# Fourier kernel on one core: first DFT of the last two x tiles by column block, first chunk read in parts, each chunk read in one transfer

## The chip, the cores and the metric

The kernel runs on one NeuronCore of a Trainium2 chip. The core has TensorE (PE, matrix products into PSUM), VectorE (DVE), ScalarE (ACT), GpSimd (POOL) and SyncE (SP, here only an issuer of DMA transfers). ACT and POOL can issue transfers too. The metric is the device time of one execution in microseconds. All data is float32; much of the matrix work is done in pairs of a rounded "high" part and a "low" rest, in the type fp32r.

## What is computed

One block of a network with two halves, on x of shape [1, 1, 4096, 640]:

```python
mod = (silu(c) @ w_mod)                 # six rows of 640: sa, ca, ga, sb, cb, gb
h = layernorm(x) * (1 + ca) + sa
x = x + ga * A(h)                       # A: spectral mixing, below
h = layernorm(x) * (1 + cb) + sb
x = x + gb * ((silu(h @ w_gate) * (h @ w_up)) @ w_down)

def A(h):
    z = rfft2(h, axes=(1, 2))           # real DFT over the 4096 positions and the height of 1
    z = z.reshape(..., 4, 160)          # four blocks of 160 columns
    hr, hi = relu(complex product of z with w1[block] + b1)
    o = complex product of (hr, hi) with w2[block] + b2
    o = sign(o) * max(abs(o) - 0.01, 0) # on the real and the imaginary part
    return irfft2(o)
```

The feed-forward half has 1728 hidden columns.

## The kernel before

The DFT over 4096 positions is split as 128 by 32. Position n is n1*32 + n2, with n1 on the 128 partitions. x is loaded as eight tiles `xas[t]`, each with four values of n2 (called rows here) of 640 columns. For each tile the kernel takes the layernorm statistics (`ln_stats`, DVE and POOL), applies them in place (`ln_apply`, shared between ACT and DVE), and multiplies with the constant matrix `fa`, the DFT over n1 (`dft_a`). That is five products for each tile, of 512 columns each. Products 0 to 3 take one row each, the first 128 columns of all four blocks; product 4 takes the last 32 columns of each block ("remainder") of all four rows. The results are copied from PSUM back over the tile (`evac_a`): row i's columns 0 to 511, and 512 to 639 for the remainders.

After that the 128 partitions hold frequencies, interleaved so that f = 0, 1, 2 picks every fourth, every fourth, and every second partition. `write_s1(t, f)` writes tile t's part f to the DRAM buffer `s1[f]`, for later reading with n2 on the partitions. f = 0 serves the frequency chunks 0 and 1, f = 1 chunks 2 and 3, f = 2 chunks 4 to 7. f = 0 and 1 are 320 KB each for a tile, f = 2 is 640 KB.

`load_g(ch, lo, hi)` reads chunk ch's rows n2 from lo to hi back, into a tile `gs[ch]` of 128 partitions (4*n2 + q) by 4 by 640; two such tiles exist. It issues one transfer for each q, so four for a chunk. Chunk 0 is read in two steps: rows 0 to 27 by POOL's queue once tile 6 is written, rows 28 to 31 by SP's queue once tile 7 is.

Each of the eight chunks then goes through these stages:

- `stage_b(ch, t)`, written b(ch,t) below: the DFT over n2 for the column block t (t = 4 is the remainders), with the table `tb`, into a bank of PSUM. `evac_b` scales the result with `ca1` and splits it into a high part (ACT) and a low part (DVE), called z. For the remainders, chunk 0 has them copied into the tile `rz` by `evac_r` block by block (ACT, DVE); other chunks write them to DRAM (`rem_high`, `rem_low`, `rem_move`) and read them back (`rem_read`).
- `stage_l1(ch, b)`, written l1(ch,b): the product with w1 for block b, bias and relu, and `tail_l1` for its remainder columns.
- `stage_l2(ch, b)`, l2(ch,b): the product with w2. DVE adds the bias and writes the tile `tt`.
- `move_x`, shrinking, and `stage_i`, the inverse DFT over n2, written to the DRAM buffer `s2` by POOL.

The loop over p = 4*ch + b sets the order: in each turn l1 of this block, b of a block of the next chunk, l2 of the block before, and the inverse of a block further back. Every engine runs its instructions in the order in which the code issues them. What sits ahead in an engine's program waits ahead, and a transfer on a queue comes behind those issued on it before.

w1 and w2 are each split into tiles a, b, c with high and low columns. `prep_weights` lists the jobs, `weights_high` does a high part (ACT for w1, POOL for w2), `weights_low` the low part (DVE). w1 has twelve jobs, done after the first DFT; w2 has six, three of whose low parts come ahead of the loop and three at the end of turn p = 0.

The tiles `w2a`, `w2b`, `w2c` lie where tiles 1, 2 and 3 of x lay, and `tt` where tiles 4 and 5 lay, so they wait for all writes of those x tiles. SP's order behind the first DFT is chunk 1's read, a table, b2, the f = 1 writes of tiles 0, 4, 5, 6, 7, chunk 2's read, a table, and the f = 2 writes of the same tiles.

`first_scale`, `remainders` and `columns` compute `ca1` (1 + ca): five DVE operations, a copy, and ten small products. `idle(n)` issues n products whose result nobody reads, to keep TensorE's clock up. There are 54 of them behind `columns` and 8 ahead of block 2 of chunk 0.

The feed-forward half follows the loop, in an order that a planner writes out when the kernel is built; the change does not touch it.

## Time and profile before

| | us |
|---|---|
| time, median of 3 runs | 1463.02 (1460.88 to 1465.1) |
| the profiled execution's own time | 1461.29 |
| its span | 1459.5 |
| PE busy | 1416.4 (97%) |
| DVE busy | 1083.6 (74%) |
| ACT busy | 785.5 (54%) |
| POOL busy | 551.7 (38%) |
| PE starts its first product | 7.94 |
| last product of the first DFT ends | 48.98 |
| first product of chunk 0 | 63.61 |

In a profile line of the timeline, the first two numbers are the start and the length in us, then come the engine (PEld is TensorE's weight load, SPq the issue of a transfer by SP), the source line, the operation, what it writes and reads, the shapes and the count; behind it, in brackets, how long the engine had been idle and what released it. Consecutive instructions of one kind are merged in a line. Matmul counts are twice the products written in the code. In the view of busy time by stretch, a DMA share of 1 means that all 16 DMA engines were busy, and the clock is the granted share of TensorE's full clock.

### The profile page before, as it was taken

How to read it: one execution, taken by the hardware profiler on the slowest of the kernel's cores; microseconds unless marked ns; L12 is line 12 of the kernel's file. 1: busy time of each engine (PE TensorE's matmuls, PEld its weight loads, DVE VectorE, ACT ScalarE, POOL GpSimd, SP SyncE). 2: the span in 40 equal slices, each digit the busy share in tenths (PEclk: the TensorE clock that was granted, in tenths of full speed). 3: DMA queues.
4: the chain of work that ended last, by engine and by line, in shares of the span. 5: the costliest groups of instructions: out<-in, count | busy, mean ns of one | idle time of the engine just before them, and what ended most of it. 6: DMA issues, size and time to landing. Idle time of an engine off the chain costs nothing.

```text
span 1459.5 us, 24171 instructions
## 1 busy us (share of the span) xinstructions
PE 1416.4 (97%) x8628; PEld 1341.4 (92%) x8628; DVE 1083.6 (74%) x1963; ACT 785.5 (54%) x1554; POOL 551.7 (38%) x646
## 2 busy tenths in 40 slices
PE   6999999998999999999999999999999999999998
PEld 2799999966888888899999999999999999999998
DVE  8568877878797788757887768888747767567775
ACT  7658888744545555544565446555434444244432
POOL 5400100044655444322544424444324545046532
PEclk9999999999999999999999999999999999999999
DMA  9967767648677988798987997877696666966652
GB/s 379 338 215 228 232 199 219 220 145 275 235 276 267 337 293 279 274 364 291 314 271 248 342 367 254 310 246 249 237 345 219 222 215 238 352 212 232 205 188 83
DMA packets 184712, 380.07 MB, mean 260 GB/s; under 512 B 22480, under 2 KB 103056, under 8 KB 182544
## 3 DMA queue, kind: packets, MB, share of 16 engines
q1 hardware_dynamic: 176080, 360.99, 71.8%
q0 software_dynamic: 6928, 14.91, 3.3%
q10 hardware_dynamic: 1584, 2.62, 0.5%
q8 instruction: 68, 1.11, 0.3%
q14 instruction: 52, 0.43, 0.1%
HBM read 263.91 MB, written 105.39 MB: 253 GB/s over the span
## 4 chain that ended last, share of the span: by engine, by line
PE 61%; DVE 8%; DMA 4%; issue 2%; ACT 2%; POOL 1%; SPq 0%; POOLq 0%; DVEq 0%; ACTq 0%
PE pd L2269 12%; PE pw L1950 8%; PE pw L1948 8%; PE pw L1949 8%; PE pd_X L2129 4%; PE pg L1813 2%; PE pg L1812 2%; PE pg L1814 2%; PE pd_Y L2129 2%; PE pw L1959 2%; PE pw L1960 2%; PE pw L1961 2%; DMA cr<-s 2%; DVE wb L1266 2%; PE pd_Z L2129 1%
## 5 line engine op out<-in xcount | busy, mean ns | idle before, releaser
L2269 PE MATMUL pd<-wdh,a 128*128 128x320 f32 x1040 | 238.9, 310 | 1.5 <-DVE a L1849 1.3
L2269 PEld LDWEIGHTS pd<-wdh,a 128*128 128x128 f32 x1040 | 176.2, 188 | 2.5 <-DVE a L1849 1.6
L1266 DVE TENSOR_TENSOR wb<-r,wb 128x512 fp32r<-128x512 f32 (+3 forms) x156 | 159.8, 1032 | 16.3 <-ACT wb L1263 14.0
L2269 PE MATMUL pd<-wdl,a 128*128 128x320 f32 x540 | 166.3, 309 | 0.0
L1948 PE MATMUL pw<-h,wt 128*128 128x384 f32 x416 | 140.8, 339 | 3.1 <-ACT s_x L1967 2.1
L1950 PE MATMUL pw<-h,wt 128*128 128x384 f32 x416 | 140.4, 338 | 0.0
L1949 PE MATMUL pw<-h,wt 128*128 128x384 f32 x416 | 139.9, 336 | 0.0
L1263 ACT ACTIVATE wb<-r 128x512 fp32r<-128x512 f32 (+3 forms) x172 | 117.9, 703 | 32.8 <-PE pw L1961 24.8
L2241 DVE TENSOR_TENSOR x<-x,pd 128x320 f32<-128x320 f32 x240 | 108.9, 477 | 35.7 <-PE pd L2269 32.1
L1950 PE MATMUL pw<-h,wb 128*128 128x384 f32 x312 | 105.1, 337 | 2.3 <-DVE wb L1266 2.3
L1948 PE MATMUL pw<-h,wb 128*128 128x384 f32 x312 | 105.5, 338 | 0.0
L1949 PE MATMUL pw<-h,wb 128*128 128x384 f32 x312 | 105.0, 337 | 0.0
L1812 PE MATMUL pg<-ht,wb 128*128 128x512 f32 x260 | 102.8, 396 | 1.3 <-ACT wb L1263 1.3
L1814 PE MATMUL pg<-ht,wb 128*128 128x512 f32 x260 | 101.7, 391 | 2.2 <-DVE wb L1266 2.2
L2269 PEld LDWEIGHTS pd<-wdl,a 128*128 128x128 f32 x540 | 101.4, 188 | 0.5
L1813 PE MATMUL pg<-ht,wb 128*128 128x512 f32 x260 | 101.5, 390 | 0.0
L742 POOL DMA_DIRECT2D s<-co x28 | 15.5, 555 | 190.8 <-ACT co L741 183.0
L1967 ACT ACTIVATE s_x<-pw 128x384 f32<-128x384 f32 x52 | 25.4, 489 | 113.6 <-PE pw L1950 112.9
L1525 POOL TENSOR_TENSOR cr<-cr,gab 128x640 f32<-128x640 f32 x28 | 47.5, 1696 | 100.5 <-DMA cr<-s 89.6
L1948 PEld LDWEIGHTS pw<-h,wt 128*128 128x128 f32 x416 | 78.3, 188 | 4.7 <-ACT s_x L1967 3.1
L1949 PEld LDWEIGHTS pw<-h,wt 128*128 128x128 f32 x416 | 78.3, 188 | 0.0
L1950 PEld LDWEIGHTS pw<-h,wt 128*128 128x128 f32 x416 | 78.3, 188 | 0.0
(335 smaller groups left out, 4079.0 us busy)
## 6 DMA issues: line engine op xcount, KB each, us to landing
wt<-td SPq DMA_DIRECT2D x104, 512.0 KB, 5.3
hs<-ho SPq DMA_DIRECT2D x52, 512.0 KB, 5.5
h<-hs SPq DMA_DIRECT2D x32, 768.0 KB, 7.9
r<-in_B_w_gate_dram SPq DMA_DIRECT2D x36, 640.0 KB, 4.8
r<-in_B_w_up_dram SPq DMA_DIRECT2D x36, 640.0 KB, 5.0
wdr<-wdd SPq DMA_DIRECT2D x21, 640.0 KB, 5.2
td<-wt SPq DMA_DIRECT2D x25, 512.0 KB, 6.0
g<-s SPq DMA_DIRECT2D x28, 320.0 KB, 5.9
```

What stands on the lines that cost most here:

```text
L1263: act.activation(wbs[t, n][:, 0, ks, e], raw[t, n][:, ks, e], AF.Copy)
L1266: (pool if onp else dve).tensor_tensor(wbs[t, n][:, 1, ks, e], raw[t, n][:, ks, e], f32(wbs[t, n][:, 0, ks, e]), op=OP.subtract)
L1525: pool.tensor_tensor(crs[r], crs[r], gab, op=OP.mult)
L1812: mm(b, wh, hh, start=(kk == 0), stop=False)
L1813: mm(b, wh, hl, start=False, stop=False)
L1814: mm(b, wl, hh, start=False, stop=(kk == 4))
L1948: mm(b, w(0, kp), a[:, kp, 0], start=start and kp == 0, stop=False, skip_group_check=not start)
L1949: mm(b, w(0, kp), a[:, kp, 1], start=False, stop=False, skip_group_check=not start)
L1950: mm(b, w(1, kp), a[:, kp, 0], start=False, stop=kp == 1, skip_group_check=not start)
L2129: mm(bk[b, i][:, :320], x, y, start=new and j == 0, stop=j == len(seq) - 1, skip_group_check=not new)
L2241: dve.tensor_tensor(x2[:, e], x2[:, e], x[0][:, :320], op=OP.add)
L2269: mm(pd[g, hf][0][:, :320], l, m, start=i == 0, stop=i == len(s) - 1 and not (last and len(gs) > 1))
```

## The change

The core of the diff (the rest is renaming and order within `prep2`):

```diff
-            def load_g(ch, lo=0, hi=32, dma=None):
+            def load_g(ch, lo=0, hi=32, dma=None, cols=(slice(0, D),)):
...
-                for q in range(4):
-                    (dma or nc.sync).dma_start(gs[ch][4 * lo + q:4 * hi:4], src[q, lo:hi])
+                for e in cols:
+                    (dma or nc.sync).dma_start(gs[ch][4 * lo:4 * hi, :, e], src[:, lo:hi, :, e].rearrange("q n j d -> n q j d"))
...
+                def write_s1(t, f, cols=None):
+                    r = slice((0, 2, 1)[f], 128, (4, 4, 2)[f])
+                    if t < 6:
+                        nc.sync.dma_start(s1[f][:, 4 * t:4 * t + 4, :], xas[t][r])
+                        return
+                    for e in cols or (slice(0, 512), slice(512, 640)):
+                        nc.sync.dma_start(s1[f][:, 4 * t:4 * t + 4, e], rst[t][r] if e.start == 512 else xas[t][r, :, e])
...
-                    elif t < 7:
-                        if t == 6:
-                            load_g(0, 0, 28, pool)
-                        for f in (1, 2):
-                            write_s1(t - 3, f)
-                    else:
-                        load_g(0, 28, 32)
+                    elif t == 5:
+                        load_g(0, 0, 20, pool)
...
-                        if i >= (4, 2, 2, 3, 2, 3, 2, 3)[t]:
+                        if i >= (4, 2, 2, 3, 2, 3, 2, 0)[t]:
...
+                def dft_c(t, i):
+                    xnr = xas[t].rearrange("p a (b e) -> p a b e", b=NB)
...
+                    mm(pa, fa, xnr[:, :, i, 0:128] if i < 4 else xnr[:, :, :, 128:160], start=True, stop=True)
+                    pas[t, i] = pa
+
+                def evac_c(t, i, eng=None):
+                    if i == 4:
+                        o = rst[t] = low_p.tile([P, 4, 128], F32, tag="e", bufs=2, name=f"rst{t}")
+                    else:
+                        o = xas[t][:, :, 128 * i:128 * i + 128]
...
+                ln_apply(7)
+                for q in ((6, 0), (6, 4), (6, 1), (7, 0), (7, 4)):
+                    dft_c(*q)
+                evac_c(6, 0)
+                evac_c(6, 4)
+                evac_c(6, 1)
+                evac_c(7, 0, dve)
+                evac_c(7, 4, dve)
+                first = (slice(0, 128), slice(512, 640))
+                rest = (slice(128, 512),)
+                write_s1(6, 0, first)
+                write_s1(7, 0, first)
+                for f in (1, 2):
+                    write_s1(1, f)
+                for q in ((6, 2), (6, 3), (7, 1), (7, 2), (7, 3)):
+                    dft_c(*q)
+                jobs = prep_weights(raws[1], w1a, w1b, w1c, True)
...
+                for job in jobs[:3]:
+                    weights_high(*job)
+                evac_c(6, 2)
+                evac_c(6, 3)
+                evac_c(7, 1)
...
+                evac_c(7, 2)
+                load_g(0, 20, 32, nc.scalar, first)
+                evac_c(7, 3)
+                for job in jobs[6:]:
+                    weights_high(*job)
+                write_s1(6, 0, rest)
+                write_s1(7, 0, rest)
+                for t in (2, 3):
+                    for f in (1, 2):
+                        write_s1(t, f)
+                load_g(0, 20, 32, None, rest)
+
+                first_scale()
                 remainders(acc0, wx0)
                 pm1 = columns(acc0, wx0)
+                idle(14)
+                for job in jobs[:4]:
+                    weights_low(*job)
                 dve.tensor_scalar(ca1, pm1[:, 0:5], 1.0, None, op0=OP.add)
-                idle(54)
-                for job in prep_weights(raws[1], w1a, w1b, w1c, True):
-                    weights_high(*job)
+                for job in jobs[4:]:
                     weights_low(*job)
...
-            pool.dma_start(bm.rearrange("p a b c -> p (a b c)"), k_bm)
...
+            prep2 = [prep2[k] for k in (0, 3, 1, 4, 2, 5)]
             for job in prep2:
                 weights_high(*job, pool)
+            pool.dma_start(bm.rearrange("p a b c -> p (a b c)"), k_bm)
...
-                pb = bank0(1 if t == 4 else 0, [P, 2, 256], f"pb{ch}_{t}")
+                pb = (ps.tile([P, 2, 256], F32, tag="p2", name=f"pb{ch}_{t}") if (ch, t) in ((0, 1), (0, 3)) else
+                      bank0(1 if t == 4 else 0, [P, 2, 256], f"pb{ch}_{t}"))
...
-            for b in range(3):
-                stage_b(0, b)
-                if b == 0:
-                    stage_b(0, 4)
-                evac_b(0, b)
-                evac_r(0, b)
-                if b == 1:
-                    idle(8)
-            for job in prep2[:3]:
-                weights_low(*job)
+            stage_b(0, 0)
+            stage_b(0, 4)
+            evac_b(0, 0)
+            evac_r(0, 0)
...
-                if b == 0:
+                if p < 2:
+                    todo = ([(0, 1), (0, 2)], [(0, 3), (1, 4), (1, 0)])[p]
+                elif b == 0:
                     todo = [(ch, 3)]
...
+                if p == 1:
+                    for job in prep2[3:]:
+                        weights_low(*job)
...
                 if p == 0:
-                    for job in prep2[3:]:
+                    for job in prep2[:3]:
                         weights_low(*job)
```

In words: the tiles 6 and 7 go through the first DFT by column block instead of by row, so that block 0 and the remainders of all their rows are ready first. These are written for f = 0 as a first part (columns 0 to 127 and 512 to 639, two transfers for a tile), the other 384 columns as a rest. Chunk 0 is read in three pieces: rows 0 to 19 by POOL after tile 5 is issued, rows 20 to 31 of the first part by ACT's queue, and their rest by SP's queue behind the f = 1 and f = 2 writes of tiles 2 and 3. A whole chunk is read in one transfer instead of four. Tile 7's layernorm is applied by DVE alone, the w1 high parts run between the evacuations, the modulation sum follows them. 14 filler products remain of 54 and 8. Chunk 0's blocks 1 to 3 move from ahead of the loop into its first two turns, and the low parts of w2 into the ends of turn 0 and the middle of turn 1.

More of the change, by code (lines that the diff above doesn't have):

```diff
@@ L420, in evac_a @@
                     for i in range(5):
-                        if t == 7 and i % 2:
-                            dve.tensor_copy(xa[:, i, 0:512], pas[t, i])
-                        elif i == 4:
+                        if i == 4:
                             act.activation(xa[:, :, 512:640], pas[t, i].rearrange("p (a e) -> p a e", a=4), AF.Copy)
@@ L430, in body @@
                 ln_apply(0)
-                for t in range(8):
-                    if t + 2 < 8:
-                        ln_stats(t + 2)
-                    if t + 1 < 8:
-                        ln_apply(t + 1)
+                for t in range(6):
+                    ln_stats(t + 2)
+                    ln_apply(t + 1)
                     dft_a(t)
-                    if t == 7:
-                        first_scale()
                     evac_a(t)
@@ L819, in body @@
                         evac_b(*q)
+                        if q[0] == 0:
+                            evac_r(*q)
                 for f, *a in sums.get(p, ()):
                     f(*a)
-                if p == 0:
-                    evac_rh(0, 3)
+                if p == 1:
+                    for job in prep2[3:]:
+                        weights_low(*job)
                 if b == 1 and ch + 1 < NCH:
```

18 lines of the change are left out of this document (14 added, 4 removed).

## The prediction

> **What bounds the kernel now.** I read the page first, then busy time by stretch of the span, then each engine's timeline from 36 to 110 us.
>
> ```profile
> span 1459.5 us, 24171 instructions
> PE 1416.4 (97%) x8628; PEld 1341.4 (92%) x8628; DVE 1083.6 (74%) x1963; ACT 785.5 (54%) x1554; POOL 551.7 (38%) x646
> ```
>
> TensorE bounds the whole: 43 us of the span are not its own. The change can only pay where it idles or runs filler, or where its clock drops.
>
> ```profile
> 10.00:15.00 5.00, 5.00 (x12) 2.00 (x11) 4.79 (x16) 3.69 (x5) 4.12 (x15) 1.00 1.07 430
> 50.00:55.00 5.00, 5.00 (x46) 5.00 (x46) 4.46 (x12) 5.00 (x14) 2.67 (x5) 1.00 0.85 316
> 55.00:60.00 5.00, 5.00 (x47) 5.00 (x46) 1.17 (x4) 0.07 (x1) 4.93 (x4) 1.00 1.05 262
> 65.00:70.00 5.00, 4.33 (x39) 4.14 (x37) 3.25 (x6) 3.01 (x6) 2.11 (x4) 1.00 1.01 411
> 70.00:75.00 5.00, 5.00 (x45) 5.00 (x44) 3.95 (x7) 4.64 (x10) 0.00 (x0) 1.00 0.14 59
> 75.00:80.00 5.00, 2.44 (x18) 2.23 (x18) 4.89 (x10) 2.93 (x8) 0.00 (x0) 0.93 0.92 289
> 80.00:85.00 5.00, 5.00 (x30) 5.00 (x30) 3.96 (x8) 1.56 (x3) 0.00 (x0) 0.73 1.01 420
> 100.00:123.00 23.00, 23.00 (x181) 23.00 (x180) 17.66 (x34) 17.11 (x34) 0.62 (x1) 1.00 0.72 194
> ```
>
> The columns after the stretch are its length, then busy time of PE, weight load, DVE, ACT and POOL, the granted clock, DMA share and GB/s. From 100 us on PE is full. Before that the DMA share is about 1 from 10 to 70 us, with one hole (0.85) and then a rest (0.14 from 70 to 75). The rates differ at equal share: 430 GB/s for the x loads, 411 for the writes of s1, 262 while chunk 0 is read from it.
>
> ```profile
> 35.63 13.35 PE L415 MATMUL pa<-xa,fa 128*128 128x512 f32 x30
> 49.67 1.05 PE L320 MATMUL pmc<-ones,acc 128*128 128x1 f32 x8 [0.69 <-ACT xa L426]
> 50.80 12.30 PE L327 MATMUL pz<-ones 128*128 128x128 f32 x108
> 63.61 2.02 PE L552 MATMUL pb<-tb,g 128*128 128x128 f32 x16 [0.50 <-DMA g<-s]
> 78.63 3.22 PE L552 MATMUL pb<-tb,g 128*128 128x128 f32 x16 [2.56 <-DVE rz L592]
> 84.46 0.52 PE L639 MATMUL pl<-z,w1a 128*128 128x256 f32 x3
> 97.00 0.47 PE L639 MATMUL pl<-rz,w1c 128*128 128x256 f32 x2 [0.17 <-issue]
> ```
>
> So PE ends the first DFT at 48.98, runs filler to 63.10 and starts chunk 0 at 63.61. After 78.63 it hardly stops again. The row at 97.00 is the first product of chunk 1 with its remainder, which comes back through DRAM; the small gap says that this landed just then.
>
> ```profile
> 39.30 11.77 SPq L346 DMA_DIRECT2D s<-xa  x10
> 54.54 5.46 SPq L309 DMA_DIRECT2D g<-s  x8
> 62.77 3.67 SPq L346 DMA_DIRECT2D s<-xa  x5
> 73.59 2.61 SPq L309 DMA_DIRECT2D g<-s  x4
> 76.88 5.67 SPq L346 DMA_DIRECT2D s<-xa  x5
> 92.64 1.76 SPq L621 DMA_DIRECT2D rz<-rzd  x4
> SPq L309 <- PE pb L552: 1.9, 2, 1.5
> 52.32 2.64 POOL L309 DMA_DIRECT2D g<-s  x4 [11.45 <-DMA s<-xa]
> ```
>
> These are DMA issues of SP (and one of POOL), and a row of SP's waits: line, releaser, us in total, times, longest. The last write of tile 7 goes out at 51.07 and SP reads it back from 54.54: 3.5 us for a write and its landing. Chunk 2's read (73.59) waits for the f=1 writes (issued 62.77 to 66.44) and for PE to release chunk 0's buffer; PE came last, by 1.5 us. The f=1 writes were thus down at about 72.1.
>
> ```profile
> 40.20 0.61 DVE L395 TENSOR_SCALAR xa<-xa,mv_a,rs_a 128x640 f32<-128x640 f32 x1 [0.93 <-POOL rs_a L197]
> 40.73 0.55 DVE L404 TENSOR_SCALAR acc<-wm,sc 128x640 f32<-128x640 f32 x1
> 41.31 3.65 DVE L406 SCALAR_TENSOR_TENSOR acc<-wm,sc,acc 128x640 f32<-128x640 f32 x4
> 49.02 1.29 DVE L422 COPY xa<-pa 128x512 f32<-128x512 f32 x2 [4.06 <-PE pa L415]
> 51.14 0.69 DVE L285 SCALAR_TENSOR_TENSOR w1a<-rm,w1a 128x512 fp32r<-128x512 f32 x1
> 55.89 0.28 DVE L285 SCALAR_TENSOR_TENSOR w1c<-rr,w1c 128x128 fp32r<-128x128 f32 x1
> 65.50 0.75 DVE L560 SCALAR_TENSOR_TENSOR z<-pb,ca,z 128x512 fp32r<-128x512 f32 x1 [9.32 <-ACT z L559]
> 77.57 1.00 DVE L592 SCALAR_TENSOR_TENSOR rz<-pb,ca,rz 32x256 fp32r<-32x256 f32 x2
> 78.60 0.83 DVE L285 SCALAR_TENSOR_TENSOR w2a<-rm,w2a 128x640 fp32r<-128x640 f32 x1
> 85.97 0.89 DVE L687 TENSOR_TENSOR tt<-pc,b2t 128x320 f32<-128x320 f32 x2 [1.32 <-DMA s<-xa]
> 39.11 1.78 ACT L397 ACTIVATE xa<-xa,nm,rs_a 128x640 f32<-128x640 f32 x2
> 42.64 0.68 ACT L424 ACTIVATE xa<-pa 128x512 f32<-128x512 f32 x1
> 65.02 1.80 POOL L280 TENSOR_SCALAR w2c<-rr 128x640 fp32r<-128x640 f32 x1
> ```
>
> Between 65 and 86 us DVE is the engine PE waits for, and at 85.97 DVE waits for the f=2 writes: tt lies where tiles 4 and 5 of x lay. The last row is the last of POOL's six w2 highs, done at 66.8.
>
> **The change, part by part.**
>
> *First DFT by columns.* A column product needs all four rows of its tile, so tile 6 starts at 39.11+1.78 = 40.9 instead of 40.1. A product is 13.35/15 = 0.89 us, the first five end at 45.3. Three applies of tile 7 move from ACT to DVE: 4 x 0.54 from 40.2, done at 42.4, in time for the fourth product. ACT copies three blocks out from 43.3, DVE two (0.65 each) until 46.0. SP's last first-part write is then out at 46.5 instead of 51.07, because the six f=1 and f=2 writes of tiles 1 to 3 no longer stand ahead of it. The other five products end at 49.8; PE loses 0.8, covered by the filler (without that cover, 0.8). A product has 512 columns as before.
>
> *Two parts, other queues.* POOL's read of 20 rows waits for tile 4's write (issued at 39.30) instead of tile 6's; behind it on POOL stand the w2 highs, which wait for tile 1's writes anyway. The first parts land 2.0 to 3.5 us later, about 49.5. ACT then issues their reads between two evacuations, at 49.8 to 51.0; what stands behind them on ACT is the last copy, hence the last rest write (out at 52.0), and half of the w1 work, which DVE does not reach before 53. SP's chunk read took 6.6 us to land under load and the remainder's 2.7 us alone:
>
> ```profile
> g<-s SPq DMA_DIRECT2D x12, 320.0 KB, 6.6
> rz<-rzd SPq DMA_DIRECT2D x8, 128.0 KB, 2.7
> ```
>
> That gives 53.7 to 57.6; I take 55.5, since two small pieces share the engines with POOL's 20 rows and the f=1 and f=2 writes of tile 1. The filler ends before it: the modulation sum (0.55+3.65, from 46.0) ends at 50.2, its columns about 1.2 later, and 14/54 of 12.30 us is 3.2, so 54.6. Chunk 0 starts at **55.5 against 63.61, 8.1 us earlier**.
>
> *DVE from there.* The w1 lows took 51.14 to 56.17 and now run from 50.5 to about 56; the first z low comes at 57.3. From the first z low to the last rz low of chunk 0, DVE needed 65.50 to 78.57, 13.1 us, for the same operations, three of the six w2 lows among them. The rest of the chunk's rows is read behind four writes on SP's queue (tiles 2 and 3, 1920 KB, 4.8 us at 411 GB/s): written at 52.0, landed at 55.5 at the earliest, read after the four writes, landed at 60 to 63. Behind this waiting read SP holds chunk 1's read (5.0 us at 262 GB/s, so there by 69), its table and the f=1 writes. Its own cover is DVE and PE on the first block until 60; what lands later is a gap. With 1 to 4 us of gaps for that, b(1,4), which needs the bank of rz, starts at 71.4 to 74.4 instead of 78.63. PE idles over 3 us ahead of it, and the clock drops as it does now after 2.56 us (0.93, then 0.73). The other bank for the second and fourth block spares PE a wait for copies that DVE's pace hides anyway: nothing.
>
> *The w2 lows put behind.* Before, three of them ran while PE did b(1,4). Now three run after chunk 1's first z low, ahead of the second layer: three of 0.8, 2.4 us added to the 5.8 us from 78.63 to 84.46. PE's l1(0,2) thus starts at 79.5 to 82.5: **2 to 5 us earlier**. POOL's w2 highs do not bind: they begin when tile 1's writes are down, 55 as now, and end near 67, and DVE's first use is near 69. (The bm read, moved behind them, is first needed at the inverse.)
>
> *What is late next.* Two things hang on DMA. tt came at 85.97, 12.4 us after chunk 2's read was issued, and the remainder at 97.0, 23.4 us after it; both sit behind that read and the f=2 writes on one queue. Chunk 2's read no longer waits for PE but for the f=1 writes, at 72.1 plus what the change adds to the queue. The bytes are the same. Added: two writes become six, in pieces of 512 B and 1536 B. At the same rate per byte that is 0; if each part costs as much as a full write (320 KB at 411 GB/s, 0.8 us) it is 3.2; I take 1.2, nearer to the first, since the bytes are the nearest row. The two first reads, in 512 B pieces, likewise 0 to 1.6; I take 0.4. DMA idle time: 53.3 to 54.5 is filled now, but 44 to 45 and 46 open: 0 within 1. One transfer for a chunk saves SP three issues of 0.65 us, which hide: SP waits for landings. Its rate is not shown: 1280 KB take 5.0 us at 262 GB/s and 3.0 at 430, the rate of 128-partition loads; I take a saving of 0.8 each, below the middle, because the source rows are scattered as before.
>
> Sum: f=1 down at 72.1+1.2+0.4-0.8 = 72.9, so chunk 2's read goes 0.7 us earlier than 73.59, lands 0.8 quicker, and tt and the remainder come 1.5 earlier. PE stands ready 2 to 5 us earlier and gives the surplus back there: **-1.5 us** by 100 us, after which PE is full and nothing changes.
>
> *A rule to weigh.* The Trainium skill's "DMA: Bandwidth & Descriptors", under "Issuing engines are not separate DMA queues", says that transfers from several engines end on the same 16 DMA engines. The row at 55 to 60 us agrees: with POOL and SP both reading, the share was 1.05 and the rate 262. By it the other queues alone gain only their place in line, which is what the sum counts.
>
> **Rivals.**
>
> *The gain goes through.* If one transfer runs at the x loads' 430 GB/s, reads save up to 2 us each, f=1 is down near 71, what hangs on chunk 2's read comes over 4 us earlier, and PE's own bound decides: 5 us, or 6 with the rest landed before 60. 1457.5. For it: the x loads' row. Against it: the scattered source. The skill's same page, "Rules for kernel authors", says 128 partitions and a MiB or more for full bandwidth, which would be this case; no trace yet shows it for these rows.
>
> *DMA later: slower.* If the small pieces cost their upper bounds (3.2 and 1.6) and the reads save nothing, f=1 lands at 76.9; at half of that, 74.5. The point is 73.59: beyond it tt and the remainder come later than before, by 0.9 to 3.3, and PE at 97 waits: 1466 at the upper end. For it: share about 1 everywhere from 36 to 70. Against it: 3.5 us of rest after 70. The skill's "DMA: Bandwidth & Descriptors", "Why a DMA increments its semaphore by 16 and not by 1", lets a DMA use the largest count up to 16 that divides both slowest dimensions: 10 engines for 20 rows, 12 for 12. The rows of before do not show on how many engines a read ran; if so, the price would be above mine.
>
> *The early start does nothing at all*: the rest lands after 66 and chunk 0's second block waits where it did. 0 to +1: 1463.5. It needs 3 us more delay than the rest's upper end.
>
> **How the numbers follow.** The profiled execution took 1461.29 us (span 1459.5), 1.7 below the median of 1463.02; the sum is a difference, so it goes on the median: 1463.0-1.5 = 1461.5. Chances: forecast 0.45 (own range 1459 to 1464), gain through 0.27, DMA later 0.21, nothing 0.07. The range takes the gain's 1457.5 and the bound of 1466.5. One 0.3% is 4.4 us, about the spread of the three runs (4.2), so what a measurement can tell: faster by more is most of the gain-through case (0.22 of its 0.27), slower by more is the part of the DMA case beyond its price, where unseen costs add to it (0.1); the same has 0.68.
>
> **What would show it.** Right: chunk 0's first product near 55.5; b(1,4) at 71 to 74 with a drop of clock; chunk 2's read near 73, released by the s1 writes and not by PE; a wait of DVE at tt or of PE at chunk 1's remainder; PE's 97.00 row 1 to 3 us earlier. Wrong: a chunk read at 400 GB/s, no wait at tt, and 5 us kept at 100 us; or chunk 2's read after 73.6.

## The result, and the profile after

The changed kernel is slower: 1474.39 us (median of 4, 1472.6 to 1476.04) against 1464.06 for the kernel before beside it, a ratio of 1.0072 [1.0050, 1.0095]; run a second time, 1.0062 [1.0041, 1.0083]. The forecast was 1461.5 with a range to 1466.5, so it is outside. The profiled execution took 1474.63 us.

First the head of the page, then busy time by stretch (length, busy time of PE, weight load, DVE, ACT and POOL, granted clock, DMA share, GB/s), of the kernel after:

```profile
span 1472.9 us, 23950 instructions
PE 1415.6 (96%) x8532; PEld 1336.5 (91%) x8532; DVE 1086.9 (74%) x1966; ACT 781.6 (53%) x1551; POOL 551.6 (37%) x643
...
45.00:50.00 5.00, 4.57 (x11) 1.71 (x9) 4.69 (x7) 4.14 (x10) 1.05 (x1) 1.00 0.63 171
50.00:55.00 5.00, 4.48 (x38) 4.32 (x38) 4.97 (x14) 2.75 (x7) 0.00 (x0) 1.00 0.86 317
55.00:60.00 5.00, 1.30 (x8) 1.03 (x8) 0.90 (x4) 0.69 (x1) 3.34 (x2) 0.83 0.93 371
60.00:65.00 5.00, 3.32 (x14) 3.06 (x14) 0.88 (x3) 0.93 (x2) 4.90 (x4) 0.50 0.51 153
65.00:70.00 5.00, 4.10 (x33) 3.86 (x33) 2.41 (x5) 3.58 (x8) 3.54 (x5) 0.99 1.03 354
75.00:80.00 5.00, 1.17 (x5) 1.21 (x6) 3.66 (x8) 1.17 (x3) 0.00 (x0) 0.88 0.53 163
85.00:90.00 5.00, 4.03 (x17) 3.77 (x17) 3.38 (x6) 0.00 (x0) 0.00 (x0) 0.56 1.00 400
```

The same view of the kernel before, two stretches that the prediction did not show:

```profile
45.00:50.00 5.00, 4.31 (x13) 1.83 (x12) 0.98 (x2) 4.16 (x9) 0.00 (x0) 1.00 0.96 399
60.00:65.00 5.00, 4.50 (x40) 4.34 (x40) 0.00 (x0) 0.22 (x1) 5.00 (x3) 1.00 1.02 311
```

TensorE is busy as long as before (1416.4 us there) with 96 filler matmuls fewer (48 products in the code), which at 12.30/108 us each are about 11 us: the rest of its products took that much longer, and it idles more. Two things stand out. The DMA engines have holes at 45 to 50 and 60 to 65: five rates times 5 us, from 45 to 70, give 6.8 MB, and 8.5 MB before. And the clock, full there before, is 0.83, 0.50 and 0.56. Next PE's timeline, then the DMA issues of ACT and SP, rows of DVE (start, duration, what, idle time before it and its releaser), and a row of SP's waits (us in total, times, longest):

```profile
51.41 3.37 PE L327 MATMUL pz<-ones 128*128 128x128 f32 x28
57.47 1.30 PE L609 MATMUL pb<-tb,g 128*128 128x128 f32 x8 [2.69 <-DMA g<-s]
61.33 2.04 PE L609 MATMUL pb<-tb,g 128*128 128x128 f32 x8 [2.56 <-DMA g<-s]
67.34 1.95 PE L609 MATMUL pb<-tb,g 128*128 128x128 f32 x16
73.11 1.05 PE L609 MATMUL pb<-tb,g 128*128 128x128 f32 x8
78.83 3.62 PE L609 MATMUL pb<-tb,g 128*128 128x128 f32 x16 [4.66 <-issue]
84.75 0.41 PE L742 MATMUL pc<-w2b,h 128*128 128x320 f32 x1 [1.57 <-DVE w2b L285]
86.28 0.63 PE L742 MATMUL pc<-w2c,r 128*128 128x320 f32 x1 [0.97 <-DVE w2c L285]
88.84 0.84 PE L696 MATMUL pl<-z,w1a 128*128 128x256 f32 x3
102.65 0.40 PE L696 MATMUL pl<-rz,w1c 128*128 128x256 f32 x2
310.26 0.78 PE L964 MATMUL py<-cfrm,et 112*128 112x320 f32 x2 [0.92 <-DMA cfrm<-s]
```

```profile
50.39 0.79 ACTq L309 DMA_DIRECT2D g<-s  x1
61.27 1.69 SPq L309 DMA_DIRECT2D g<-s  x2
70.06 0.77 SPq L353 DMA_DIRECT2D s<-rst  x1
76.41 0.60 SPq L309 DMA_DIRECT2D g<-s  x1
77.72 1.00 DVE L649 SCALAR_TENSOR_TENSOR rz<-pb,ca,rz 32x256 fp32r<-32x256 f32 x2
83.21 0.75 DVE L617 SCALAR_TENSOR_TENSOR z<-pb,ca,z 128x512 fp32r<-128x512 f32 x1 [4.49 <-ACT z L616]
83.88 0.81 DVE L285 SCALAR_TENSOR_TENSOR w2b<-rm,w2b 128x640 fp32r<-128x640 f32 x1
87.98 0.49 DVE L744 TENSOR_TENSOR tt<-pc,b2t 128x320 f32<-128x320 f32 x1 [0.55 <-DMA s<-xa]
...
SPq L309 <- DMA g<-s: 3.4, 1, 3.4
```

Chunk 0 starts 6.1 us earlier (57.47 against 63.61), but b(1,4) comes at 78.83, as before (78.63). From there the kernel falls behind: l1(0,2) at 88.84 against 84.46, and the product with chunk 1's remainder at 102.65 against 97.00. That +5.65 stays: just behind the inverse transform, at the first product with `cfrm`, it is 310.26 against 303.99 in the kernel before, +6.3:

```profile
303.99 0.70 PE L910 MATMUL py<-cfrm,et 112*128 112x320 f32 x2
```

These are rows of one profile. In a second one of the same kernel (run 15 below) the early start is smaller and is lost sooner, at the second block, b(0,1), and b(1,4) is 4.5 us later than before:

```profile
59.68 2.05 PE L609 MATMUL pb<-tb,g 128*128 128x128 f32 x8 [4.36 <-DMA g<-s]
71.08 2.53 PE L609 MATMUL pb<-tb,g 128*128 128x128 f32 x16
83.15 3.35 PE L609 MATMUL pb<-tb,g 128*128 128x128 f32 x16 [4.66 <-issue]
```

**What SP waits for ahead of the rest rows.** The row of SP's waits above says that the read at 61.27 was released by another read of chunk 0, and not by the write that it reads back. The trace has the semaphores and landings. The transfers of SP and ACT go round eight semaphores between them, and each waits until the one that last had its semaphore has landed. The read of the rest rows got the semaphore of ACT's second read. Its own two writes were down at 57.07 and 57.72, ACT's read only at 61.19; in the second profile they were down at 59.28 and 59.94 and ACT's read at 63.43, and SP's read went at 63.51. So the last 3.5 us of this wait come from the slow read on ACT's queue. In runs 1 and 2 below the write came last (58.67 and 59.73, reads at 58.72 and 59.78), and 60 to 65 has 252 and 287 GB/s instead of 153.

### The profile page after: what moved, and what is told of

It reads as the page before. It is cut to its first block, busy times and chain, and to the rows that moved or that the text cites. A ratio compares the mean times of both kernels' runs of the same rounds, so it can differ in the third digit from the quotient of the medians.

```text
span 1472.9 us, 23950 instructions
## 1 busy us (share of the span) xinstructions
PE 1415.6 (96%) x8532; PEld 1336.5 (91%) x8532; DVE 1086.9 (74%) x1966; ACT 781.6 (53%) x1551; POOL 551.6 (37%) x643
## 3 DMA queue, kind: packets, MB, share of 16 engines
q1 hardware_dynamic: 178044, 361.12, 71.4%
## 4 chain that ended last, share of the span: by engine, by line
PE 66%; issue 10%; DVE 9%; DMA 8%; ACT 4%; POOL 3%; SPq 1%; ACTq 0%; POOLq 0%; DVEq 0%
PE pd L2323 12%; PE pw L2002 7%; PE pw L2004 7%; PE pw L2003 7%; PE pd_X L2183 4%; DMA cr<-s 3%; PE pg L1866 3%; PE pg L1868 3%; PE pg L1867 3%; PE pc L742 2%; PE pd_Y L2183 2%; PE pl L696 2%; PE pw L2013 2%; PE pw L2014 2%; PE pw L2015 2%
```

## The experiments

The table has one row a run. MB: the five rates from 45 to 70 us times 5 us. Read: SP's issue of chunk 2's read. Remainder: PE's first product with chunk 1's remainder. All three are of one profile each, and the two profiles of the changed kernel are 2.3 us apart in the read and 1.3 us in the remainder, so a difference of that size between two rows can be chance. The ratio is to the kernel before beside it.

| run | MB | read, us | remainder, us | ratio [95%] |
|---|---|---|---|---|
| before | 8.5 | 73.59 | 97.00 | 1 |
| after | 6.8 | 76.41 | 102.65 | 1.0072 [1.0050, 1.0095] |
| after again | 6.2 | 78.74 | 103.95 | 1.0062 [1.0041, 1.0083] |
| 1 first parts read on SP | 7.4 | 76.23 | 100.21 | 1.0039 [1.0022, 1.0057] |
| 2 w2 lows early | 7.3 | 76.48 | 100.15 | 1.0026 [1.0008, 1.0043] |
| 3 filler | 7.5 | 75.42 | 99.19 | 1.0010 [0.9994, 1.0026] |
| 4 before, one transfer | 8.6 | 73.39 | 96.91 | 0.9997 [0.9977, 1.0017] |
| 5 = 2, writes forward | 6.6 | 77.02 | 101.04 | 1.0062 [1.0043, 1.0081] |
| 6 = 1 and 2 | 7.3 | 76.06 | 99.22 | 1.0047 [1.0030, 1.0064] |
| 7 = 1, 2, 5, filler | 6.7 | 78.83 | 102.47 | 1.0025 [1.0008, 1.0042] |
| 8 = 7, remainder on POOL | 6.4 | 77.85 | 101.26 | 1.0033 [1.0017, 1.0049] |
| 9 = 2, f=1 ahead | 7.1 | 76.71 | 100.67 | 1.0053 [1.0037, 1.0069] |
| 10 = 6, f=1 ahead | 7.4 | 76.25 | 99.78 | 1.0030 [1.0015, 1.0045] |
| 11 = 10, filler, remainder on POOL | 7.5 | 75.67 | 99.35 | 1.0016 [1.0004, 1.0029] |
| 12 before, filler, remainder on POOL | 8.5 | 73.85 | 98.02 | 1.0013 [1.0002, 1.0023] |
| 13 before, less filler | 8.2 | 75.48 | 99.43 | 0.9997 [0.9981, 1.0013] |
| 14 = 2, filler of 3 | 6.6 | 78.22 | 102.49 | 1.0018 [1.0004, 1.0033] |
| 16 = 7, f=1 ahead | 7.6 | 74.99 | 98.23 | 1.0024 [1.0011, 1.0036] |
| 17 writes as before | 5.2 | 81.75 | 105.92 | 1.0039 [1.0024, 1.0053] |
| 18 = 16, filler, remainder on POOL | 7.4 | 75.36 | 99.03 | 1.0012 [0.9997, 1.0027] |

**One part at a time (1 to 4).** Theory A: TensorE's own side, late first reads, the place of the w2 lows and the clock. Theory B: the DMA queue.

```diff
-                load_g(0, 20, 32, nc.scalar, first)
+                load_g(0, 20, 32, None, first)
```

> The changed kernel, but chunk 0's first-part reads go out on SP's queue instead of ACT's. Theory A (packet turns): on ACT's queue the 512 B packets take turns with 10240 B writes of tiles 1 to 3 on SP's queue, one for one, so the second read lands at 61.2, 10 us after its issue. On SP's queue they stand in line between tile 1's writes and the rest: they land near 54, block 0's remainder product starts by 57 instead of 61.3, l1(0,0) near 59, chunk 1's first product 3 to 5 us earlier than 78.8, the product with chunk 1's remainder (turn 4, 102.65) 2 to 5 us earlier; about 1470. Theory B (the total of DMA work sets it): turn 4 within 1 us of 102.65, time unchanged at 1474.

1468.17 us: better than Theory A said (about 1470), and not Theory B's 1474. Both halves of chunk 0's first block now come together:

```profile
57.58 3.35 PE L609 MATMUL pb<-tb,g 128*128 128x128 f32 x16 [2.14 <-DMA g<-s]
65.90 2.05 PE L609 MATMUL pb<-tb,g 128*128 128x128 f32 x16 [0.83 <-DMA g<-s]
```

The remainder block no longer trails by 3.9 us, but the second block still waits for the rest rows until 65.90. So b(1,4) comes at 77.49, only 1.3 us earlier and not 3 to 5; the remainder, at 100.21, is 2.4 us earlier, as Theory A had it.

```diff
                 for q in todo:
+                    if q == (1, 4):
+                        for job in prep2[3:]:
+                            weights_low(*job)
                     stage_b(*q)
...
-                if p == 1:
-                    for job in prep2[3:]:
-                        weights_low(*job)
```

> The changed kernel, but the three w2 low parts of turn 1 go ahead of chunk 1's first products instead of behind them, into the time (78.7 to 83.2) in which DVE idles. Theory A (front on DVE and PE): the waits of 1.6 and 1.0 us ahead of the second layer go, l1(0,2) starts 2 to 4 us earlier than 88.84, turn 4 as well; 1470 to 1472. Theory B (DMA): tt still comes at 88, turn 4 within 1 us of 102.65, 1474.

1467.65 us, better than Theory A's 1470 to 1472: the interval lies below the changed kernel's first one and touches its second. PE's timeline:

```profile
78.10 3.75 PE L609 MATMUL pb<-tb,g 128*128 128x128 f32 x16 [4.66 <-issue]
84.45 0.52 PE L696 MATMUL pl<-z,w1a 128*128 128x256 f32 x3
89.50 0.70 PE L742 MATMUL pc<-w2a,h 128*128 128x320 f32 x3 [1.49 <-DVE tt L744]
100.15 0.47 PE L696 MATMUL pl<-rz,w1c 128*128 128x256 f32 x2 [1.59 <-DMA rz<-rzd]
```

From b(1,4) to l1(0,2) it is 6.35 us, not 10.01, and l1(0,2) stands where it did before. But PE then waits for tt and for the remainder, 3.1 us together: a second bound, behind the first.

The third run fills PE's gaps with products that nobody reads:

```diff
-                idle(14)
+                idle(25)
...
             stage_b(0, 0)
+            idle(10)
             stage_b(0, 4)
...
                 for q in todo:
+                    if q == (1, 4):
+                        idle(18)
                     stage_b(*q)
```

> The changed kernel with filler products in PE's three gaps: 25 instead of 14 ahead of chunk 0, 10 between its first two products, 18 ahead of chunk 1's first. Theory A (clock): the granted clock stays at 1.0 from 55 to 95 us, chunk 1's first products take 2.0 instead of 3.6 us, l1(0,2) starts 3 to 5 us earlier, turn 4 as well: 1469 to 1471. Theory B (DMA): the clock stays up but turn 4 does not move by more than 1 us: 1474.

1465.86 us, far better than expected: the mean clock over its 10 executions is 0.997 where the changed kernel had 0.990. In its profile no clock drop comes before 84 us. That profile is of an execution 4.5 us below the median (1461.40), so its rows show more than the usual gain.

The fourth gives the kernel before only the single transfer for chunks 1 to 7:

```diff
+                if hi - lo == 32:
+                    nc.sync.dma_start(gs[ch], src.rearrange("q n j d -> n q j d"))
+                    return
                 for q in range(4):
```

> The kernel before, with chunks 1 to 7 read in one transfer each and nothing else changed. If one transfer is as good or better (its packets took 113 ns against 110 to 211 in four): chunk 2's read still goes at 73.6, lands up to 1 us earlier, turn 4 at 96 to 97, time 1462 to 1464, the same. If one transfer is part of the loss: chunk 2's tt and remainder later, 1465 or more.

1464.28 us, no difference: the transfers' form does not cost.

**Do they add? (5 to 8).** 5 moves writes on SP's queue; 6 is 1 and 2 together; 7 is all of it with filler; 8 moves chunk 1's remainder to POOL's queue as well.

```diff
                         load_g(0, 0, 20, pool)
+                        for f in (1, 2):
+                            write_s1(1, f)
...
-                for f in (1, 2):
-                    write_s1(1, f)
+                for t in (2, 3):
+                    for f in (1, 2):
+                        write_s1(t, f)
                 for q in ((6, 2), (6, 3), (7, 1), (7, 2), (7, 3)):
```

For 7, `idle(23)` and, ahead of b(1,4), `idle(18)`; for 8, on top of it:

```diff
-                nc.sync.dma_start(rzd[ch, ...
+                (pool if ch == 1 else nc.sync).dma_start(rzd[ch, ...
...
-                    nc.sync.dma_start(f32(r[32 * q ...
+                    (pool if ch == 1 else nc.sync).dma_start(f32(r[32 * q ...
```

> Changed kernel with the w2 lows ahead of b(1,4) (as in the experiment with early lows), and the f=1 and f=2 writes of tiles 2 and 3 put ahead of the rest writes, those of tile 1 ahead of the first parts. Theory B (what is left over after the lows is the DMA hole from 43 to 48 us: 17.9 MB moved by 50 us against 19.4 before, and 28.4 against 29.8 by 85 us, 1.4 MB or 3.3 us at 411 GB/s): by 50 us at least 18.8 MB are moved, chunk 2's read goes near 74 instead of 76.5, the wait of DVE at tt falls from 4.3 to under 2.5 us, PE's wait for chunk 1's remainder (100.15) moves to 97 to 98.5, and the median falls 2 to 3 us below the early-lows kernel's 1467.7, to 1465. Rival A (what is left over is the lateness of the first-part reads on TensorE's side): those reads now share the engines with more 10 KB packets, chunk 0's first product comes 1 to 3 us later than 59.2, and the median is 1468 to 1470.

> Changed kernel with both earlier edits: the first parts read on SP's queue, and the w2 lows ahead of b(1,4). Rival A (both are delays on TensorE's side, and add): each alone took 6 to 7 us off 1474.4; together 1462 to 1464, PE's l1(0,2) near 82.5 and no wait for chunk 1's remainder over 0.5 us. Theory B (behind them stands one floor, the remainder's arrival through the DMA queue): l1(0,2) comes earlier than 84.5 but PE then waits at the remainder or at tt, w1c of chunk 1 still at 99.5 to 100.5 as in the early-lows kernel, and the median stays at 1466.5 to 1468.5.

> Changed kernel with the writes forward, the first parts read on SP's queue, the w2 lows ahead of b(1,4), and filler before chunk 0 (23 instead of 14 steps) and before b(1,4) (18). Theory B: the floor is the remainder, 97 to 98.5 us, so 1463 to 1465.5 however early chunk 0 starts, with a wait of 1 us or more of PE at the remainder. Rival A: everything on TensorE's side is mended, chunk 0 starts near 57.5 and the 5 to 6 us of the early start come through: 1457 to 1460.

> The same with chunk 1's remainder written and read back on POOL's queue instead of SP's, where it stands behind the f=2 writes and three small loads. Theory B: the remainder comes before PE needs it, the wait at chunk 1's remainder goes, tt becomes the floor: w1c of chunk 1 at 94 to 96.5, median 1460 to 1463, 2 to 3 us below the kernel with it on SP's queue. Rival A (the remainder's place in the queue does not decide): the same time as that kernel within 1 us.

5: 1472.29 us (four executions), above both expectations; Theory B as put there is wrong. 45 to 50 rose to 285 GB/s, but 60 to 65 fell to 106: the hole moved. 6: 1468.28, as Theory B had it: no sum, w1c at 99.22 (a little earlier than its 99.5 to 100.5, in the fastest execution of six, 1461.04). 7: 1467.10, above both expectations. 8: 1467.25, no gain from POOL's queue.

**The second hole (9 to 12).** 9 to 11 issue three f=1 writes ahead of the read of chunk 0's rest rows (on the kernels named in the table); 12 is 4 with `idle(9)` ahead of b(1,4) and the remainder on POOL's queue.

```diff
+                for t in (0, 4, 5):
+                    write_s1(t, 1)
                 load_g(0, 20, 32, None, rest)
```

> The kernel with early w2 lows, and the f=1 writes of tiles 0, 4 and 5 moved ahead of the read of chunk 0's rest rows, so that SP holds less behind that waiting read. Theory C (chunk 1's read and the f=1 writes stand on SP behind a read that waits until 61 us for a write to land; before, the same read went out at 54.5; the engines run dry from 60 to 64, 22.2 MB against 23.9 by 65 us): at least 23.0 MB by 65 us, the last f=1 write issued before 69 instead of 70.8, chunk 2's read at 73 to 75 instead of 76.5, DVE's wait at tt under 3 us instead of 4.3, chunk 1's remainder product at 97.5 to 99 instead of 100.15; median 1465 to 1466.5. Rival (the pieces and the waits of each issue for the transfer eight before it decide): chunk 2's read stays at 76 to 77 and nothing moves by over 0.5 us. Second rival (the writes only delay the rest rows): b(0,1) 1 to 2.5 us later than 66.6, and the median 1469.

> The same with the first parts read on SP's queue as well. Theory C: as there, chunk 2's read at 72.5 to 74.5 instead of 76.1, and the remainder's product at 96.5 to 98.5 instead of 99.2; median 1463 to 1466. If the order of the queue does not decide: as the kernel with early lows and the read on SP, 1468.

> The same with filler before chunk 0 (23 steps instead of 14) and before b(1,4) (18 steps), and chunk 1's remainder on POOL's queue. Theory C: no half clock until 95 us, the remainder is no longer the floor but tt is, l1(1,0) with its remainder at 94.5 to 97.5; median 1460 to 1464. Rival (only the remainder's own way counts, 18.5 us from b(1,4) as in the kernel before): 1463 to 1465.

> The kernel before with one transfer for chunks 1 to 7, nine steps of filler ahead of b(1,4), and chunk 1's remainder written and read on POOL's queue. In the kernel before, the 2.56 us wait ahead of b(1,4) is followed by 3.4 us at half clock, worth 1.7 us; where that drop was missing, PE waited 1.87 us at the remainder instead. If both are the last waits there, PE's row of chunk 1's remainder comes at 94.5 to 96 instead of 97.0, and the median 1 to 2.5 us below the kernel before. If tt or the remainder still binds: within 0.5 us of it.

9: 1471.63 us; 60 to 65 rises to 324 GB/s, but 65 to 70 falls to 279 and chunk 2's read stays at 76.71, as its first rival had it; b(0,1) comes at 68.57, 2.0 us later than in run 2, as the second had it; the median is above all three. 10: 1467.88, a miss too. 11: 1465.67, above both expectations. 12: 1465.70, a miss: its row of the remainder is at 98.02, with PE waiting 2.11 us there.

**Clock, and a second look (13 to 15).** 13 is the kernel before with `idle(14)` for `idle(54)`; 14 is the early lows with the filler of 3; 15 is the changed kernel once more.

> The kernel before with 14 instead of 54 steps of filler after the modulation columns: TensorE idles about 9 us ahead of chunk 0, as the changed kernel idles ahead of its first products, and nothing else changes. Clock theory (a gap of some us is followed by half-clock spells, and these are what the changed kernel lost most by): half clock from about 58 on, chunk 0's products and the first layer at half rate, b(1,4) 1 to 3 us later than 78.63, and, if early half clock also brings more of it later, a mean clock of 0.993 to 0.995 instead of 0.9975 and a median 3 to 6 us above the kernel before. Rival (the half clock falls on waits and costs nothing where DMA and VectorE bind): within 1 us of the kernel before.

1462.49 us: the median as the rival had it. Busy time by stretch, and a row of PE:

```profile
55.00:60.00 5.00, 0.00 (x0) 0.00 (x0) 1.30 (x5) 0.20 (x1) 4.93 (x5) 0.82 0.94 251
60.00:65.00 5.00, 0.63 (x3) 0.67 (x4) 0.00 (x0) 0.00 (x0) 5.00 (x4) 0.50 1.04 293
65.00:70.00 5.00, 5.00 (x31) 4.85 (x31) 1.61 (x3) 2.26 (x4) 2.82 (x4) 0.66 1.03 396
...
80.53 2.05 PE L552 MATMUL pb<-tb,g 128*128 128x128 f32 x16 [2.56 <-DVE rz L592]
```

About 5 us of clock is missing here (5 us times 0.18, 0.50 and 0.34), but TensorE worked for only 0.63 of the first 10 us, so about 2 us of it fall on products (half clock from 64.4 to 68.4). In this profile b(1,4) does come 1.9 us later, as the clock theory had it, and the remainder 2.4 us; this execution took 1466.64, above the median. Over the 10 executions the mean clock is 0.993 against 0.997 and the median is the same; the interval leaves room for 1.9 us. So a drop that falls mostly on idle time cost too little to see in the median.

> The changed kernel with the filler of the earlier experiment (25, 10 and 18 steps) and the w2 lows ahead of b(1,4). If lows and clock are separate losses: b(1,4) near 77.3, l1(0,2) near 82.5 with no wait for w2b or w2c, then the floor of tt and of chunk 1's remainder (99 to 100); median 1464 to 1466, within 0.3% of the kernel before. If they add in full (no floor): 1459 to 1461. If the lows count for nothing beside the filler: 1465.9.

1466.92 us: no better than filler alone (3). In its profile DVE waits 7.0 us for the f=2 writes before tt, and PE 4.63 us behind it.

> The changed kernel itself, unchanged, for a second profile beside these. If the later stages' part belongs to the kernel: median 1473 to 1476, and from the inverse transform's end to the end 1159 us or more again (1162.1 in the first profile, 1153.8 in the kernel before). If it belonged to that execution: 1153 to 1157 there, and the median 1470 to 1472.

1472.51 us, between the two cases. The row that stood at 303.99 and 310.26:

```profile
310.86 0.78 PE L964 MATMUL py<-cfrm,et 112*128 112x320 f32 x2 [0.43 <-DMA cfrm<-s]
```

From this row to the end of the span it is 1157.5 us, against 1162.6 in the first profile and 1155.5 in the kernel before. (The two lengths in the expectation are counted from another point.) The loss up to this row comes back, +6.9; of the 7.1 us behind it in the first profile, 2.0 do.

**Both holes, and the writes put back (16 to 18).** 16 is 7 with the three f=1 writes ahead of the rest rows' read. 17 puts the six writes of tiles 1 to 3 ahead of the first parts, as before, with the SP read, early lows and filler (30 and 18 steps):

```diff
+                    elif t == 4:
+                        for f in (1, 2):
+                            write_s1(1, f)
                     elif t == 5:
                         load_g(0, 0, 20, pool)
+                        for k in (2, 3):
+                            for f in (1, 2):
+                                write_s1(k, f)
```

> The kernel with the writes of tiles 1 to 3 forward, the first parts read on SP, early w2 lows and filler (23 and 18), and the f=1 writes of tiles 0, 4 and 5 ahead of the read of chunk 0's rest rows: both holes filled. If bytes not moved decide: at least 24.8 MB by 70 us (25.9 before, 23.6 with the writes forward alone), chunk 2's read at 74 to 76 instead of 78.8, tt at 86 to 88 instead of 90.2, and the median 1464 to 1466. If it is the two waits for writes to land, which no order fills: chunk 2's read at 77 or later and the median 1467 or more.

> The changed kernel with the six writes of tiles 1 to 3 ahead of the first parts, as in the kernel before, the first parts read on SP, early w2 lows and filler (30 and 18). If bytes decide: about 19.2 MB by 50 us, the first parts land later and chunk 0 starts at 59.5 to 61.5, chunk 2's read at 74 to 75.5, tt at 85.5 to 87.5, and the median 1462.5 to 1465.5: level with the kernel before, the early start gone. If the split read and its waits decide by themselves: chunk 2's read at 76 to 78 all the same and the median 1466 to 1468.

16: 1464.71 us, and chunk 2's read and tt (86.49) as expected where both holes count; PE's row:

```profile
98.23 0.48 PE L698 MATMUL pl<-rz,w1c 128*128 128x256 f32 x2 [2.12 <-DMA rz<-rzd]
```

17: 1468.26 us, the second case and beyond it: by 50 us as many bytes are moved as before, but then SP's queue holds nothing to fill its waits with. SP's issues and two stretches:

```profile
51.52 0.69 SPq L353 DMA_DIRECT2D s<-rst  x1
59.65 1.90 SPq L309 DMA_DIRECT2D g<-s  x2
61.64 1.32 SPq L353 DMA_DIRECT2D s<-xa  x2
65.88 1.48 SPq L309 DMA_DIRECT2D g<-s  x2
81.75 0.63 SPq L309 DMA_DIRECT2D g<-s  x1
...
55.00:60.00 5.00, 4.39 (x40) 4.20 (x38) 3.36 (x6) 0.00 (x0) 5.00 (x3) 1.00 0.37 86
65.00:70.00 5.00, 4.13 (x21) 3.89 (x22) 1.23 (x3) 1.25 (x3) 0.00 (x0) 0.69 0.47 103
```

The read of the first parts waits until 59.65 for writes issued at 51.52, the read of the rest from 62.96 to 65.88, and chunk 2's read goes out 8 us later than before. This is the plainest view of what a split read-back does to a queue: two reads that each wait for their write at its head (landed at 59.63 and 65.81), where the kernel before had one. It is not the whole cause of the time: with the latest read and remainder of all rows, run 17 is still nearer to the kernel before than the changed kernel is.

18 is 16 with `idle(36)` and the remainder on POOL's queue.

> The kernel with both holes filled, with 36 steps of filler ahead of chunk 0 instead of 23 (its first product came at 61.1) and chunk 1's remainder on POOL's queue. If the remainder is the last wait there: TensorE's product with chunk 1's remainder at 95.5 to 97.5 instead of 98.2, and the median 0 to 2 us below that of the kernel before. If tt (86.5) or the state of the DMA engines binds: 97.5 to 99, and the median 1 to 3 us above it.

18: 1464.72 against 1463.90 us, and the product with the remainder at 99.03 with 2.72 us of waiting: nearer the second case. It is level with the kernel before within its interval; no version beat that kernel.

## Why the prediction was wrong

*"What bounds the kernel now"*: right, and in the end the loss arose there, between 45 and 104 us, where TensorE waits.

*First DFT by columns*: right. The filler ended at 54.78 (54.6 forecast), and the first part's reads were issued at 48.9 to 51.2 (49.8 to 51.0).

*Two parts, other queues*: 55.5 forecast, 57.47 measured, and the block's other half, b(0,4), only at 61.33. The step took both pieces to land together. Run 1 shows that ACT's queue split them. The trace's packets say how; counts by start in each us, SP's queue left, ACT's right, 512 B pieces and their time:

```
us   SP's queue                      ACT's queue
52   12 of 10240 B (408 ns)          32 of 512 B (30 ns)
53   48 of 1536 B, 19 of 10240 B     5 of 512 B
55   69 of 1536 B, 18 of 10240 B     134 of 512 B (27 ns)
58   37 of 10240 B (387 ns)          13 of 512 B
60   24 of 10240 B (385 ns)          7 of 512 B
```

A 512 B packet takes 27 to 30 ns, but near 60 us some 10 of them pass in 1 us beside 30 large ones: the queues seem to take turns by packet, not by byte, which no run tests alone. In run 1, on SP's own queue, 303 of the 384 start within 1 us (56 to 57). Something else slows the transfers of this stage: of a write's sixteen landings, six come early and ten late while POOL's 20 rows are read (tile 1's f=2 write, issued at 47.31: 50.72 to 50.86 and 55.27 to 56.40; before, one issued at 44.47 had all sixteen from 48.80 to 50.24). That fits the prediction's remark under "DMA later" that a read of 20 rows may use ten engines, and each read of 12 rows shows twelve landings. Every variant of the changed kernel reads 20 and 12 rows, so what this costs is untested.

*DVE from there*: the step that failed first. It had the rest rows at 60 to 63 and b(1,4) at 71.4 to 74.4, and let the read of the rest rows wait for its write alone. SP issued it at 61.27, held by ACT's second read, and it landed at 66.0 (68.2 in the second profile). The second block came at 67.34 (71.08), against 66.30 before, and b(1,4) at 78.83 (83.15). What held the second block in the first profile was the first block's other half, at 61.33; right behind it stood the rest rows, for which PE waits in run 1. In the second profile the first layer of block 0 ran at half clock besides (0.50 from 60 to 70). So the early start ended at the second block. The rival "the early start does nothing at all" had this, with 0.07, and its point, rest rows after 66, was reached.

*The w2 lows put behind*: 2.4 us were counted for three operations; from b(1,4) to l1(0,2) it became 10.0 us instead of 5.83, so 4.2 (8.6 in the second profile, to 91.75). The term left out what DVE waits for ahead of them: they stand behind z low of chunk 1's first block, which waited 4.49 us for ACT and that for b(1,0), at half clock (0.50 from 79 to 82). Run 2 puts them ahead of it: 6.35 us.

*"The clock drops as it does now"*: mis-sized. Over all executions the mean clock is 0.990 (0.997 before). Where it drops matters more than how long: most of run 13's drop falls on idle time, while in the changed kernel the spells lie on b(1,4), the second layer and l1(0,2), where PE sets the pace (88.84 to 92.26 for six groups that took 84.46 to 86.36 before). Filler alone took back 0.6% (run 3), the most of all single edits. The drops follow the gaps of 2.69 and 2.56 us (0.83 and 0.50 from 55 to 65) and of 4.66 (0.88, later 0.56); but in the profile of run 4 a gap of 2.56 us ahead of b(1,4) has no drop behind it, so such a gap does not always bring one.

*What is late next*: the step that the other floor rests on. "f=1 down at 72.1+1.2+0.4-0.8 = 72.9" and "DMA idle time: 0 within 1" made chunk 2's read 0.7 earlier; it went at 76.41, 2.8 later, and in the second profile at 78.74. The 72.1 was a misreading of the kernel before: the longest wait of 1.5 us is a later read's. From 60 to 80 us alone the view says

```profile
SPq L309 <- PE pb L552: 0.4, 1, 0.4
```

and in the trace the last f=1 write was down at 73.14. With that figure the prediction's own sum gives 73.9, later than 73.59 and not earlier, and 1.0 of the forecast 1.5 us is gone. In the changed kernel the f=1 writes were down at 76.18, 3.0 us later. The term for single transfers was not the fault (run 4). That for pieces no run tests alone; of the f=1 writes, seven transfers where there were five, the sixth waited 2.1 us for chunk 1's read to land and free its semaphore (issued at 69.41), while the DMA engines had other work (354 GB/s from 65 to 70). The largest part that the runs show is the idle time: 1.7 MB fewer from 45 to 70 us are 4 us at 411 GB/s. The prediction had written that SP holds chunk 1's read and the f=1 writes behind the waiting rest read, and then did not count it. In the table the read comes later as fewer MB are moved, from 8.6 MB and 73.39 to 5.2 and 81.75: 2.5 us per MB, all within 1.4 us of that line, which is about what 411 GB/s needs for a MB (2.4 us). The Trainium skill's "DMA: Bandwidth & Descriptors", under "Anatomy of one DMA", says that the engines themselves do not wait on semaphores, the issuing sequencer does; run 17 agrees, with 86 and 103 GB/s while SP waits.

*The rivals*: "DMA later" had the right point (73.59) and direction; its means, the price of small pieces, was not what the runs show, and its remark on the engines stayed untested. It was given 0.21, and slower as a whole 0.10.

So two bounds were both late by 100 us: TensorE's side by 5.65 us, and behind it the DMA side by 2 to 3 (97.00 against 99.2 to 100.2 in runs 2, 3 and 6). That fits single edits that gave back so much and did not add.

**What stays open.** The stage to the inverse transform explains 6.3 and 6.9 us; the medians differ by 10.3 and 8.9. The stages behind it run unchanged code, but their length in single profiles went from 1153 to 1163 us; whether the changed kernel lengthens them by 2 to 4 us on average was not settled. For the same reason the ratios of runs that differ by less than 0.2% are not ranked here: 7 and 16 differ by 4 us at the remainder and not in the ratio, and run 17, latest of all there (105.92), has 1.0039. Over the kernels with the change the ratio goes rather with the mean clock of all executions: the four slowest ratios (after, again, 5 and 9) have a mean clock of 0.990 to 0.992, the four fastest (3, 18, 11 and 14) 0.996 to 0.997. That does not show the clock as the cause, since waits lower it too.

## What to carry to other kernels

A read that must wait for a write to land holds all that stands behind it on its queue, and what it waits for may be another transfer altogether: look up its releaser, here a read on another queue with the same semaphore. Before splitting such a round trip in two, list what the engines will have to move during each wait, and count the megabytes that they will not move, not only the ones that were added. When small operations are put behind a matrix product, price the instruction that is ahead of them in the same in-order queue, and the clock that follows the gap.

## What was not expected of the hardware

Half clock with next to no price: run 13 ran 55 to 70 us at 0.82, 0.50 and 0.66, and its median lost nothing (0.9997 [0.9981, 1.0013]). The Trainium skill's "TensorE: Matmul & The Clock Gate", in its "Terms", puts the penalty at about the throttled time times the missing share, which over the whole stretch would be an estimate of about 5 us. TensorE was idle for 9.4 of these 15 us, so only about 2 us are left where it worked: the profile agrees with these (b(1,4) 1.9 us later), and the median, with its room for 1.9 us, does not settle them.

And small packets beside large ones on another queue: 27 to 33 ns each, and yet 384 of them needed from 51 to 61 us, and held a read on SP's queue until the last was down.
